# A two-layer decode kernel: projections on the uncentred x, and sums across partitions as two bf16 terms

## The chip, the cores and the metric

The kernel runs on one core of one Trainium2 chip. The metric is the device time of one execution in microseconds (us). Each version is timed in several runs and the median is given. One more execution is recorded by the hardware profiler; its views are what this text calls the profile and the trace.

## What is computed

Four residual steps on x, which has 4 batch rows (one token each) of 512 numbers. Attention A and gated unit B alternate twice, with the same weights and the same K and V both times:

```python
def _layernorm(x, axis=-1, eps=1e-5):
    m = jnp.mean(x, axis=axis, keepdims=True)
    v = jnp.var(x, axis=axis, keepdims=True)
    return (x - m) / jnp.sqrt(v + eps)
...
x = x + A(_layernorm(x))      # q = x @ wq; 32 query heads on 8 K/V heads, 4096 keys, head size 128
x = x + B(_layernorm(x))      # sigmoid(x @ w_gate) * (x @ w_up) @ w_down, inner size 1792
x = x + A(_layernorm(x))
x = x + B(_layernorm(x))
```

Everything is bf16 in memory. K and V are 33.6 MB each and do not fit on the core, so V is read twice and K once, with some of it read again.

## The kernel before

**Layers and batches.** Layer 0 and layer 1 are interleaved: for each batch row b the kernel does attention of layer 0, then `cross` (out-projection result, residual, norm, gated unit, residual, norm), then the queries of layer 1, then the scores of layer 1 on the K tiles that are still in memory. The values of layer 1 follow later, when V comes by a second time. The gated unit of layer 1 is done once for all four rows, in the last `cross`.

**Loads.** All come from SP's queue in the order of a string (line 385): k is two halves of K tiles, V and v a V tile (two halves) for layer 0 and layer 1, r the halves of K that were given up and are read again (`again`, line 386: 3, 3, 2 and 4 halves for the four rows), digits and letters a to d, g, u, w are pieces of the weights, which stay in memory. A half is 512 KB and sits in one of 22 ring slots. A slot comes free when the last reader of its half is done. SP waits for that before it issues the next load.

**K and the scores.** DVE transposes each half of K in place (line 502), 1.234 us each. A batch row's 16 halves, less those read again, stay in their slots from the scores of layer 0 to those of layer 1. Scores (line 515) need the queries spread into block form: PE permutes them (line 478), then four ACT operations write `qbd` (line 491). The softmax takes maxima on DVE (lines 532 to 551), exponentials on ACT (line 556), and transposes the result on PE and ACT into `pt_sb` (line 575).

**Values.** PE multiplies V's halves with `pt_sb` (line 603), 16 matmuls a half. DVE scales by the inverse denominators `winv` into `oT` (line 612). The denominators come from ACT's row sums: two POOL operations (580, 584), a float32 matmul against a column of ones (587), and a reciprocal (589). `y_proj` multiplies by wo.

**The norm.** `layer_norm` and `rstd` (lines 419 to 458): the row sums are summed across partitions by a float32 matmul with a column of -1/512 (`stat`, line 416), DVE adds this negative mean to x and writes bf16 `xT` (440), ACT squares with the mean as bias (445), a second float32 matmul sums across partitions, DVE scales (452), and POOL takes the power -0.5 (456). The matmuls of the gated unit or of q_proj (line 469) take xT. The factor 1/sqrt is applied later, on the results.

**Order of the work.** A planner (`_Sched.place`) lists the operations of each engine by estimated durations and priorities and writes the order out. Every engine then runs its list strictly in that order and waits by semaphores. The durations in `S.put` are the planner's; the priorities are the constants of line 472.

Of the kernel before, what the change touches and what calls it, by code (L numbers as in the profile page):

```python
# [202 lines left out]
def bass_interleave_layers__gqa_block_cached__glu_gated_glu__decode_kernel(nc, A_x, A_k, A_v, A_wq, A_wo, B_x, B_wg, B_wu, B_wd, out):  # L203
# [44 lines left out]
    xT = sb("xT", [P, KD], bf)  # L248
    xTj = sb("xTj", [P, B, KD], bf)
    gs = sb("gs", [P, NF * B])  # L250
    hT = sb("hT", [P, NF * B], bf)
    cols = sb("cols", [P, 64])
    xsum = cols[:, 0:8]
    nmean = cols[:, 8:12]
# [4 lines left out]
    pos, neg, ones, nbias = (cols[:, i:i + 1] for i in range(32, 36))  # L259
# [12 lines left out]
    dsel = sb("dsel", [P, 16])  # L272
# [19 lines left out]

    def col(t):
        return t[:, 0:1].broadcast_to([P, P])
# [23 lines left out]
    for key, ap, v in (("neg", neg, -1.0 / D), ("pos", pos, 1.0 / D), ("mhalf", mhalf, -0.5), ("ones", ones, 1.0)):  # L318
        S.put("dve", lambda e, ap=ap, v=v: e.memset(ap, v), 0.08, 0, writes=[key])
    for name, t in (("mask_a", mask_a), ("sel_den", sel_den)):  # L320
        S.put("pool", lambda e, t=t: e.memset(t[:], 0.0), 0.15, 0, writes=[name, "pl"])
    for g in range(4):
        m = mask_a[32 * g:32 * g + 32, g * R:(g + 1) * R]
        S.put("pool", lambda e, m=m: e.memset(m, 1.0), 0.1, 0, reads=["mask_a"], writes=["mask_a", "sel_den", "pl"])
        v = sel_den[:].rearrange("p (g h) -> p g h", g=4)[:, g, :]
        for a in range(4):
            S.put("pool", affine(sel_den, v, [[-1, R]], -(32 * g + 4 * a), 1.0), 0.2, 0, reads=["sel_den"], writes=["sel_den", "pl"])
# [7 lines left out]
    again = (((6, 1), (7, 0), (7, 1)), ((6, 1), (7, 0), (7, 1)), ((7, 0), (7, 1)), ((6, 0), (6, 1), (7, 0), (7, 1)))  # L335
# [49 lines left out]
    order = 'kk01kk23VkkVVkkVbcdVgaVVVuwrkkkkvkkVvkkVVVVVVVvvvvkvvkrkkvkkkvVkVVVVVVVvvvvkvvrkkkkvkkkvVVVVVVVVvvvvvrvvvvvvvvv'  # L385
    again = (((6, 1), (7, 0), (7, 1)), ((6, 1), (7, 0), (7, 1)), ((7, 0), (7, 1)), ((6, 0), (6, 1), (7, 0), (7, 1)))
# [27 lines left out]
    def stat(c, si, nb, w, wkey, prio):  # L414
        S.put(
            "pe", mm(G_ps[:, c:c + nb], col(w), xsum[:, si:si + nb]), 0.58, prio, reads=[f"xsum{si}", wkey], writes=["G"],
        )

    def layer_norm(x, xkey, xT_ap, xT_key, nb, prio):
        if nb > 1:  # L420
            S.put(
                "dve", lambda e: e.tensor_reduce(xsum[:, 0:nb], x, AX.X, ALU.add), 0.2, prio, reads=[xkey], writes=["xsum0"],
            )
        stat(0, 0, nb, neg, "neg", prio)
        if nb > 1:
            S.put(
                "dve", lambda e: e.tensor_tensor(xw[:], x, bcast(G_ps[:, 0:nb], KD), ALU.add), 0.2, prio,
                reads=[xkey, "G"], writes=["xw"],
            )
            S.put("dve", lambda e: e.tensor_copy(xT_ap, xw[:]), 0.17, prio, reads=["xw"], writes=[xT_key])  # L430
            S.put(
                "dve", lambda e: e.tensor_tensor(xw[:], xw[:], xw[:], ALU.mult), 0.17, prio, reads=["xw"], writes=["xw"],
            )
            S.put(
                "dve", lambda e: e.tensor_reduce(xsum[:, 4:4 + nb], xw[:], AX.X, ALU.add), 0.2, prio, reads=["xw"],
                writes=["xsum4"],
            )
        else:
            S.put(
                "dve", lambda e: e.tensor_scalar(xT_ap, x, G_ps[:, 0:1], None, op0=ALU.add), 0.17, prio,  # L440
                reads=[xkey, "G"], writes=[xT_key],
            )
            S.put("dve", lambda e: e.tensor_copy(nmean[:, 0:1], G_ps[:, 0:1]), 0.15, prio, reads=["G"], writes=["nmean"])  # L443
            S.put(
                "act", lambda e: e.activation(gs[:, 0:KD], x, ACTF.Square, bias=nmean[:, 0:1], accum_out=xsum[:, 4:5]), 0.4,  # L445
                prio, reads=[xkey, "nmean"], writes=["gs", "xsum4"],
            )

    def rstd(mult, rs, rs_key, nb, prio):
        stat(4, 4, nb, pos, "pos", prio)  # L450
        S.put(
            "dve", lambda e: e.tensor_scalar(vpe[:, 0:nb], G_ps[:, 4:4 + nb], mult, mult * eps, op0=ALU.mult, op1=ALU.add),  # L452
            0.17, prio, reads=["G"], writes=["vpe"],
        )
        S.put(
            "pool", lambda e: e.tensor_tensor(rs, vpe[:, 0:nb], mhalf[:, 0:nb], ALU.pow), 0.6, prio,  # L456
            reads=["vpe", "mhalf"], writes=[rs_key, "pl"],
        )

    def q_proj(s, xT_of, n, dst, dkey, prio, xkey):  # L460
        fns = []
        for h in range(16):
            hh = 16 * s + h
            for k in range(KD):
                c0 = (hh % 8) * DH
                fns.append(mm(
                    M_ps[:, h * n:(h + 1) * n], wq[:, hh // 8, k, c0:c0 + DH], xT_of(k), k == 0, k == KD - 1,
                ))
        S.put("pe", fns, 2.0, prio, reads=[xkey, f"wq{2 * s}", f"wq{2 * s + 1}"], writes=["M"])
        S.put("act", lambda e: e.activation(dst, M_ps[:, 0:16 * n], ACTF.Copy), 0.25, prio, reads=["M"], writes=[dkey])  # L470

    PS0, PS1, PL0, PL1, PV0, PV1, PK0, PK1, PDEN, PEV = (1.24, 0.52, 0.5, 1, 1.15, 0.7, 2.1, 2.1, 0.9, 0.6)
# [54 lines left out]
    def softmax(u, rs, rs_key, prio):  # L527
# [11 lines left out]
        S.put("dve", lambda e: e.transpose(tr[:], ml[:]), 0.22, prio, reads=["ml0", "ml1"], writes=["tr"])  # L539
# [28 lines left out]
        for t4 in range(4):  # L568
# [15 lines left out]
            "pool", lambda e: e.tensor_scalar(dsel[:], sel_den[:], ls[:, 0:1], None, op0=ALU.mult), 0.6, pd,  # L584
            reads=["ls0", "sel_den"], writes=["dsel", "pl"],
        )
        S.put("pe", mm(M_ps[:, 480:496], col(ones), dsel[:]), 0.6, pd, reads=["dsel", "ones"], writes=["M"])
# [41 lines left out]
    def cross(l, b, prio):  # L629

        last = l == 1
        nb = B if last else 1
        xres = xj[:] if last else x0[:, b, :]
        y = Y_ps[:, 0:nb * KD]
        u = Y_ps[:, 64:64 + NF * nb]
        g = G_ps[:, 64:64 + NF * nb]
        rs = rs_h[:, 0:nb]
        if last:
            x, xkey, xt = xj[:], "xj", xTj
            S.put(  # L640
                "dve", lambda e: e.tensor_tensor(xj[:], y.rearrange("p (b k) -> p b k", b=nb), xj[:], ALU.add), 0.2, prio,
                reads=["Y", "xj"], writes=["xj"],
            )
            layer_norm(x, xkey, xTj[:], "xTj", nb, prio)
            xk, xtkey = (lambda k: xTj[:, :, k]), "xTj"
        else:
            x, xkey = xj[:, b, :], "xj"
            S.put(
                "dve", lambda e: e.scalar_tensor_tensor(
                    out=x, in0=y, scalar=1.0, in1=xres, op0=ALU.mult, op1=ALU.add, accum_out=xsum[:, 0:1],  # L650
                ), 0.3, prio, reads=["Y", "x0"], writes=["xj", "xsum0"],
            )
            layer_norm(x, xkey, xT[:], "xT", 1, prio)
            xk, xtkey = (lambda k: xT[:, k:k + 1]), "xT"
        for w, key, dst, bkey in ((wg, "wg", g, "G"), (wu, "wu", u, "Y")):
            for f0, f1 in ((0, 3), (3, 6), (6, 10), (10, NF)):
                fns = []
                for f in range(f0, f1):
                    for k in range(KD):
                        fns.append(mm(  # L660
                            dst[:, f * nb:(f + 1) * nb], w[:, k, f * P:(f + 1) * P], xk(k), k == 0, k == KD - 1,
                        ))
                S.put("pe", fns, 0.033 * len(fns), prio, reads=[xtkey, key], writes=[bkey])
                if w is wg and f1 == 6:
                    rstd(4.0, rs, "rs_h", nb, prio)
        if last:
            S.put(
                "dve", lambda e: e.tensor_tensor(
                    gs[:].rearrange("p (f b) -> p f b", b=nb), g.rearrange("p (f b) -> p f b", b=nb),
                    rs.unsqueeze(1).broadcast_to([P, NF, nb]), ALU.mult  # L670
                ), 0.2, prio, reads=["G", "rs_h"], writes=["gs"],
            )
            S.put("act", lambda e: e.activation(gs[:], gs[:], ACTF.Tanh), 0.25, prio, reads=["gs"], writes=["gs"])
        else:
            S.put(
                "act", lambda e: e.activation(gs[:, 0:NF], g, ACTF.Tanh, scale=rs), 0.22, prio, reads=["G", "rs_h"],
                writes=["gs"],
            )
        S.put(
            "dve", lambda e: e.scalar_tensor_tensor(  # L680
                out=hT[:, 0:NF * nb], in0=gs[:, 0:NF * nb], scalar=1.0, in1=u, op0=ALU.add, op1=ALU.mult
            ), 0.2, prio, reads=["gs", "Y"], writes=["hT"],
        )
        fns = []
        for j in range(KD):
            for f in range(NF):
                fns.append(mm(
                    y.rearrange("p (b k) -> p b k", b=nb)[:, :, j], wd[:, f, j * P:(j + 1) * P],
                    hT[:, f * nb:(f + 1) * nb], f == 0, f == NF - 1,
                ))  # L690
        S.put("pe", fns, 1.85, prio, reads=["hT", "wd"], writes=["Y"])
        if not last:
# [159 lines left out]
```

## Time and profile before

| what | value |
|---|---|
| median of 11 runs | 340.29 us (339.05 to 342.87) |
| the profiled execution | 341.07 us |
| its span, first to last instruction | 339.3 us |
| mean granted clock of TensorE | 0.58 |
| HBM read | 120.85 MB |
| busy: PE, DVE, ACT, POOL | 214.9, 147.2, 71.8, 20.4 us |
| K transposes (L502) | 76, 92.8 us in all |
| float32 matmul pairs for sums across partitions | 36, 352 to 366 ns a matmul |

The profile has a page and several views. The page's row of slices cuts the span into 40 equal parts. Groups of instructions give the line, the engine, what is written from what, shapes, a count and the mean time. The chain of waits follows the work that ended last back to its releasers. The timeline lists instructions in order of time; in square brackets stands the idle time of the engine before an instruction, and what ended it. "issue" is idle time in which the engine waited for nothing that the profile shows. L301 is the line of the helper that makes most matmuls, so those are told apart by the tile they write: G_ps, Y_ps and M_ps for the sums, the gated unit and the projections.

### The profile page before, as it was taken

To read this page: it belongs to the slowest core of one execution; us is meant where nothing else is said; L and a number is where in the kernel's file an instruction comes from. 1 tells how busy PE (TensorE), PEld (TensorE's weight loads), DVE (VectorE), ACT (ScalarE), POOL (GpSimd) and SP (SyncE) were. 2 spreads that over 40 slices of the span, in tenths; PEclk is the share of its full clock that TensorE was granted. 3 is DMA by queue.
4 is the path that set the end of the run, shared out by engine and by line. 5 is a ranking of instruction groups with operands and counts; after the bars stand their busy time and mean duration, and the time that the engine had idled before them with its cause. 6 is when DMAs were issued, how large, how long until landed. Compare 5 with 4: busy or idle time off the path is not lost.

```text
span 339.3 us, 11560 instructions
## 1 busy us (share of the span) xinstructions
PE 214.9 (63%) x5202; PEld 162.8 (48%) x5202; DVE 147.2 (43%) x321; ACT 71.8 (21%) x192; POOL 20.4 (6%) x74
## 2 busy tenths in 40 slices
PE   1154633174676668679667586876755868698786
PEld 1123412164633347678223466774332657573676
DVE  6284460000887761012899520134997301155111
ACT  1013103000235303002163230001632200014300
POOL 6100000000001000000000000000000000000001
PEclk9995555555567755555575555555965555557555
DMA  7999999999959999998999999989899999999920
GB/s 216 401 394 410 409 372 381 388 405 371 404 186 375 412 409 408 410 405 312 340 375 396 409 393 409 409 294 352 287 399 412 407 409 408 405 357 308 410 87 4
DMA packets 38626, 121.62 MB, mean 358 GB/s; under 512 B 3504, under 2 KB 9392, under 8 KB 38576
## 3 DMA queue, kind: packets, MB, share of 16 engines
q1 hardware_dynamic: 38544, 120.87, 93.7%
q8 instruction: 41, 0.67, 0.8%
q14 instruction: 9, 0.07, 0.1%
q10 hardware_dynamic: 32, 0.00, 0.0%
HBM read 120.85 MB, written 0.00 MB: 356 GB/s over the span
## 4 chain that ended last, share of the span: by engine, by line
DMA 47%; PE 26%; SPq 11%; DVE 6%; issue 6%; ACT 3%; DVEq 0%; ACTq 0%
DMA ring<-in_A_v_cache_dram 29%; DMA ring<-in_A_k_cache_dram 18%; SPq L341 9%; PE O_ps L603 7%; PE Y_ps L301 5%; PE M_ps L301 5%; PE S_ps L515 5%; PE G_ps L301 3%; DVE ring L502 3%; PE PT_ps L301 2%; SPq L362 1%; DVE ml L532 1%; ACT qbd L491 1%; ACT p_sb L556 1%; ACT p_sb L564 0%
## 5 line engine op out<-in xcount | busy, mean ns | idle before, releaser
L502 DVE STREAM_TRANSPOSE ring<-ring 128x1024 int32<-128x1024 int32 x76 | 92.8, 1234 | 33.2 <-DMA ring<-in_A_k_cache_dram 32.6
L603 PE MATMUL O_ps<-pt_sb,ring 128*128 128x4 bf16 x2048 | 68.2, 167 | 49.9 <-DMA ring<-in_A_v_cache_dram 31.5
L603 PEld LDWEIGHTS O_ps<-pt_sb,ring 128*128 128x128 bf16 x2048 | 63.2, 105 | 61.7 <-DMA ring<-in_A_v_cache_dram 30.8
L515 PE MATMUL S_ps<-ring,qbd 128*16 128x512 bf16 x512 | 53.2, 560 | 8.2 <-DVE ring L502 6.5
L612 DVE TENSOR_TENSOR oT<-O_ps,winv 128x12 bf16<-128x12 f32 (+3 forms) x29 | 4.9, 169 | 73.6 <-PE O_ps L603 73.6
L556 ACT ACTIVATE p_sb<-S_ps,cols 128x512 bf16<-128x512 f32 x32 | 24.7, 773 | 56.3 <-DVE cols L551 48.3
L532 DVE TENSOR_REDUCE ml<-S_ps 128x1 f32<-128x512 f32 x32 | 21.4, 670 | 21.7 <-PE S_ps L515 21.7
L301 PE MATMUL Y_ps<-oT,wo 128*128 128x1 bf16 (+1 forms) x640 | 20.3, 166 | 10.6 <-DMA wo<-in_A_wo_dram 6.9
L515 PEld LDWEIGHTS S_ps<-ring,qbd 128*16 128x16 bf16 x512 | 12.3, 105 | 28.4 <-issue 13.8
L301 PEld LDWEIGHTS Y_ps<-oT,wo 128*128 128x128 bf16 x640 | 18.7, 104 | 12.6 <-DMA wo<-in_A_wo_dram 7.0
L491 ACT ACTIVATE qbd<-M_ps,mask_a 128x64 bf16<-128x64 f32 x64 | 20.1, 314 | 18.5 <-PE M_ps L301 17.0
L445 ACT ACTIVATE gs<-xj,cols 128x4 f32<-128x4 f32 x8 | 2.4, 297 | 83.7 <-DVE cols L443 83.7
L301 PE MATMUL M_ps<-xT,wq 128*128 128x1 bf16 x512 | 15.2, 165 | 6.2 <-issue 3.8
L301 PE MATMUL PT_ps<-ident_b,p_sb 128*128 128x64 bf16 x128 | 10.5, 231 | 12.4 <-ACT p_sb L556 12.4
L301 PEld LDWEIGHTS M_ps<-xT,wq 128*128 128x128 bf16 x512 | 14.5, 104 | 6.8 <-issue 3.9
L301 PEld LDWEIGHTS PT_ps<-ident_b,p_sb 128*128 128x128 bf16 x128 | 7.1, 118 | 17.0 <-ACT p_sb L556 14.3
L456 POOL TENSOR_TENSOR cols<-cols 128x1 f32<-128x1 f32 (+1 forms) x10 | 6.6, 656 | 137.7 <-DVE cols L452 137.5
L564 ACT ACTIVATE p_sb<-PT_ps 128x512 bf16<-128x512 f32 x16 | 9.6, 598 | 17.8 <-PE PT_ps L301 17.8
L301 PE MATMUL G_ps<-cols 128*128 128x1 f32 (+1 forms) x40 | 11.4, 354 | 3.0 <-DVE xj L694 1.0
L580 POOL TENSOR_TENSOR cols<-cols 128x1 f32<-128x1 f32 x16 | 3.1, 193 | 168.9 <-ACT p_sb L556 168.9
L301 PE MATMUL PT_ps<-p_sb,ident_b 128*32 128x128 bf16 x256 | 10.0, 298 | 5.1 <-ACT p_sb L564 3.7
L575 ACT ACTIVATE pt_sb<-PT_ps 128x512 bf16<-128x512 f32 x16 | 9.5, 595 | 15.9 <-PE PT_ps L301 15.9
(75 smaller groups left out, 158.9 us busy)
## 6 DMA issues: line engine op xcount, KB each, us to landing
ring<-in_A_v_cache_dram SPq DMA_DIRECT2D x128, 512.0 KB, 10.4
ring<-in_A_k_cache_dram SPq DMA_DIRECT2D x76, 512.0 KB, 10.3
wq<-in_A_wq_dram SPq DMA_DIRECT2D x4, 1024.0 KB, 13.3
wo<-in_A_wo_dram SPq DMA_DIRECT2D x4, 1024.0 KB, 15.6
wg<-in_B_w_gate_dram SPq DMA_DIRECT2D x1, 1792.0 KB, 11.4
wu<-in_B_w_up_dram SPq DMA_DIRECT2D x1, 1792.0 KB, 17.1
wd<-in_B_w_down_dram SPq DMA_DIRECT2D x1, 1792.0 KB, 21.5
x<-in_A_x_dram SPq DMA_DIRECT2D x1, 4.0 KB, 1.7
```

Source lines behind the costliest of these rows:

```text
L301: return lambda e: e.matmul(o, lhsT=l, rhs=r, start=start, stop=stop)
L341: return e.dma_start(ring[t.slot], t.src.rearrange("(p t) d -> p (t d)", p=P)[:, q * TS:(q + 1) * TS])
L456: "pool", lambda e: e.tensor_tensor(rs, vpe[:, 0:nb], mhalf[:, 0:nb], ALU.pow), 0.6, prio,
L491: "act", lambda e, a=a: e.activation(qbd[u % NQB][:].rearrange("p g n x -> p (g n) x")[:, :, 4 * a:4 * a + 4], M_ps[:, 256:320].rearrange( ...
L502: return e.transpose(v, v)
L515: return e.matmul(bank[32 * gi:32 * gi + 16, :], lhsT=qbd[u % NQB][:, gi, nn, :], rhs=kt[:, :, nn // 2, :, nn % 2], start=nn == 0, stop=nn ...
L532: "dve", lambda e, q=q: e.tensor_reduce(ml[:, q:q + 1], S_ps[banks[q]][:], AX.X, ALU.max, negate=True), 0.65,
L556: "act", lambda e, q=q: e.activation(p_sb[:, 4 * q:4 * q + 4, :].rearrange("p c x -> p (c x)"), S_ps[banks[q]][:], ACTF.Exp, bias=nbias, s ...
L564: "act", lambda e: e.activation(pt1.rearrange("p c g a h -> p (c g a h)"), PT_ps[:], ACTF.Copy), 0.65, prio,
L575: "act", lambda e: e.activation(pt_sb[pi][:].rearrange("p q c g h -> p (q c g h)"), PT_ps[:], ACTF.Copy), 0.65,
L603: return e.matmul(O_ps[:, gi * R:(gi + 1) * R], lhsT=ring[tile.slot][:, (t % HT) * DH:(t % HT + 1) * DH], rhs=pt_sb[pi][:, t % 4, t // 4, ...
L612: "dve", lambda e: e.tensor_tensor(o, O_ps[:, c0:c1], winv[pi][:, c0:c1], ALU.mult), 0.2, PEV,
```

## The change

1. **Projections on the uncentred x.** `xT` holds x itself in bf16, written straight from the matmul result by `add_y`; a second operation writes the float32 x with its sum. For batch row 0 a second column of ones goes through wg, wu and wq, which gives the column sums of the weights (`csum`). `centre` then adds (negative mean) x (column sums) to a projection's result: on the gate, on the up projection and on the queries. The last cross does the same for four rows with broadcasts.
2. **The variance** is taken about the mean of the norm before (`nm`), and corrected by the squared difference of the two means (`dd`).
3. **Sums across partitions** are split: a bf16 copy and the bf16 rest, two matmuls against a bf16 matrix of -1/512. The denominators use it too (`sel_den` holds -512), with two more POOL operations. In a cross, one statistic of both sums stands behind the wg matmuls.
4. **The spread of layer 1's queries** is one DVE product instead of four ACT operations; the copy of q from PSUM on ACT becomes `centre` on DVE.
5. **The order of loads** and the halves read again: 0, 3, 3 and 1 instead of 3, 3, 2 and 4. Three priorities change.

```diff
-    xT = sb("xT", [P, KD], bf)
+    xT = sb("xT", [P, KD, 2], bf)
...
-    for key, ap, v in (("neg", neg, -1.0 / D), ("pos", pos, 1.0 / D), ("mhalf", mhalf, -0.5), ("ones", ones, 1.0)):
+    for key, ap, v in (("negb", negb[:], -1.0 / D), ("mhalf", mhalf, -0.5), ("xT", xT[:], 1.0)):
...
-    order = 'kk01kk23VkkVVkkVbcdVgaVVVuwrkkkkvkkVvkkVVVVVVVvvvvkvvkrkkvkkkvVkVVVVVVVvvvvkvvrkkkkvkkkvVVVVVVVVvvvvvrvvvvvvvvv'
-    again = (((6, 1), (7, 0), (7, 1)), ((6, 1), (7, 0), (7, 1)), ((7, 0), (7, 1)), ((6, 0), (6, 1), (7, 0), (7, 1)))
+    order = '1k0kkkk23VkkVVkVVbdgacVVVuwrvkkkkkkVvkkVVVVVVVvkvvvvkrvkkkkkvvVkVVVVVVVvkvvvvrkkkkkVvvkvkVVVVVVVvvvvvvvvrvvvvvv'
+    again = ((), ((6, 1), (7, 0), (7, 1)), ((5, 1), (6, 1), (7, 1)), ((7, 1),))
...
+    def stat(c, n, prio, reads):
+        hi, lo = (t[:, c:c + n] for t in xs16)
+        S.put("dve", lambda e: e.tensor_copy(hi, xsum[:, c:c + n]), 0.15, prio, reads=reads, writes=["xs_hi"])
+        S.put(
+            "dve", lambda e: e.tensor_tensor(lo, xsum[:, c:c + n], hi, ALU.subtract), 0.15, prio, reads=reads + ["xs_hi"],
+            writes=["xs_lo"],
+        )
+        fns = [mm(G_ps[:, c:c + n], negb[:], hi, True, False), mm(G_ps[:, c:c + n], negb[:], lo, False, True)]
+        S.put("pe", fns, 0.1, prio, reads=["xs_hi", "xs_lo", "negb"], writes=["G"])
...
+    def add_y(b, y, scal, skey, res, rkey, mi, prio):
+        S.put(
+            "dve", lambda e: e.scalar_tensor_tensor(
+                out=xT[:, :, 0], in0=y, scalar=scal, in1=res, op0=ALU.mult, op1=ALU.add,
+            ), 0.2, prio, reads=["Y", rkey] + skey, writes=["xT"],
+        )
+        S.put(
+            "dve", lambda e: e.scalar_tensor_tensor(
+                out=xj[:, b, :], in0=y, scalar=scal, in1=res, op0=ALU.mult, op1=ALU.add, accum_out=xsum[:, 0:1],
+            ), 0.3, prio, reads=["Y", rkey] + skey, writes=["xj", "xsum0"],
+        )
+        S.put(
+            "act", lambda e: e.activation(
+                xw[:, 0, :], xj[:, b, :], ACTF.Square, bias=nm[mi][:, b:b + 1], accum_out=xsum[:, 1:2]
+            ), 0.4, prio, reads=["xj", f"nm{mi}"], writes=["xw", "xsum4"],
+        )
+
+    def norm(b, mi, mult, rs, rs_key, prio):
+        stat(0, 2, prio, ["xsum0", "xsum4"])
+        new, old = nm[1 - mi][:, b:b + 1], nm[mi][:, b:b + 1]
+        S.put("dve", lambda e: e.tensor_copy(new, G_ps[:, 0:1]), 0.15, prio, reads=["G"], writes=[f"nm{1 - mi}"])
...
+    def centre(o, okey, src, skey, n, mi, b, prio):
+        if b == 0:
+            S.put("dve", lambda e: e.tensor_copy(csum[n][:], src[:, :, 1]), 0.2, prio, reads=[skey], writes=[f"cs{n}"])
+        S.put(
+            "dve", lambda e: e.scalar_tensor_tensor(
+                out=o, in0=csum[n][:], scalar=nm[mi][:, b:b + 1], in1=src[:, :, 0], op0=ALU.mult, op1=ALU.add,
+            ), 0.2, prio, reads=[skey, f"nm{mi}", f"cs{n}"], writes=[okey],
+        )
...
-    PS0, PS1, PL0, PL1, PV0, PV1, PK0, PK1, PDEN, PEV = (1.24, 0.52, 0.5, 1, 1.15, 0.7, 2.1, 2.1, 0.9, 0.6)
+    PS0, PS1, PL0, PL1, PV0, PV1, PK0, PK1, PDEN, PEV = (1.24, 0.52, 0.5, 1, 1.15, 0.9, 2.1, 2.1, 0.72, 1.8)
...
-            "pool", lambda e: e.tensor_scalar(dsel[:], sel_den[:], ls[:, 0:1], None, op0=ALU.mult), 0.6, pd,
-            reads=["ls0", "sel_den"], writes=["dsel", "pl"],
-        )
-        S.put("pe", mm(M_ps[:, 480:496], col(ones), dsel[:]), 0.6, pd, reads=["dsel", "ones"], writes=["M"])
+            "pool", lambda e: e.tensor_scalar(dfull[:], sel_den[:], ls[:, 0:1], None, op0=ALU.mult), 0.6, pd,
+            reads=["ls0", "sel_den"], writes=["dfull", "pl"],
+        )
+        S.put("pool", lambda e: e.tensor_copy(dsel[0][:], dfull[:]), 0.6, pd, reads=["dfull"], writes=["dsel0", "pl"])
...
+        fns = [mm(M_ps[:, 480:496], negb[:], dsel[i][:], i == 0, i == 1) for i in range(2)]
+        S.put("pe", fns, 0.1, pd, reads=["dsel0", "dsel1", "negb"], writes=["M"])
...
+    def cross(b, prio):
+        y = Y_ps[:, 0:KD]
+        rs = rs_h[:, 0:1]
+        add_y(b, y, 1.0, [], x0[:, b, :], "x0", 0, prio)
+        n = 2 if b == 0 else 1
+        g, u = glu(n, lambda k: xT[:, k, 0:n], "xT", lambda: norm(b, 0, 4.0, rs, "rs_h", prio), prio)
+        centre(gs[:, 0:NF], "gs", g, "G", "wg", 1, b, prio)
...
+        centre(us_sb[:, 0:NF], "us", u, "Y", "wu", 1, b, prio)
+        down(1, prio)
+        add_y(b, y, rs, ["rs_h"], xj[:, b, :], "xj", 1, prio)
+        norm(b, 1, float(DH), rs_q[1][:, b:b + 1], f"rs_q1{b}", prio)
...
-            q_spread(q2T[s][:], f"q2T{s}", u, prio, ('act', 'act')[1])
+            q_spread(q2T[s][:], f"q2T{s}", u, prio, ('act', 'dve')[1])
```

`glu` holds the wg and wu matmuls as before, with the statistic between them. `last_cross` is the four-row form of `cross`: two operations write `xTj` and `xj`, then come six DVE operations for the sums, `between` with the statistic and the correction, and products with broadcast `csum` and means.

## The prediction

> **What bounds the kernel now.** I read three views of the profile in this order: the page's slices with its DMA queues, the chain that ended last in order of time, then the timeline around one hand-over between the layers. First the page:
>
> ```profile
> DMA  7999999999959999998999999989899999999920
> GB/s 216 401 394 410 409 372 381 388 405 371 404 186 375 412 409 408 410 405 312 340 375 396 409 393 409 409 294 352 287 399 412 407 409 408 405 357 308 410 87 4
> q8 instruction: 41, 0.67, 0.8%
> ```
>
> The transfers run at 405 to 412 GB/s over most of the span, so the load stream is the first bound: a half tile of K or V (0.524 MB) costs 1.27 us at 412 GB/s. The dips come at four places, once per batch, and the last 14 us have no loads at all. The busy time of the stretches shows what the dips cost:
>
> ```profile
> 92.00:106.00 14.00, 11.66 (x182) 5.47 (x182) 11.52 (x19) 6.41 (x20) 1.08 (x3) 0.64 0.73 249
> 154.00:172.00 18.00, 13.80 (x308) 9.33 (x309) 10.56 (x20) 4.89 (x16) 0.55 (x1) 0.55 0.93 317
> 224.00:246.00 22.00, 16.45 (x382) 11.20 (x379) 14.09 (x26) 7.76 (x25) 1.08 (x3) 0.67 0.87 299
> 302.00:312.00 10.00, 9.03 (x153) 4.07 (x150) 3.32 (x10) 3.07 (x9) 0.53 (x2) 0.67 0.94 303
> ```
>
> The columns are the stretch, its length, the busy time of PE, PEld, DVE, ACT and POOL, PE's clock, DMA share and GB/s. Time lost against 412: 14 x (1 - 249/412) = 5.5 us, then 4.2, 6.0 and 2.6. These are hand-overs: batch b's K halves sit in the 22 ring slots until its layer-1 scores, and those wait for cross(0,b) and q_proj. Until then SP waits for a slot, and since it issues in list order, one load without a slot holds all behind it. After the last hand-over the chain holds no load at all:
>
> ```profile
> 274.55 11.44 DMA ring<-in_A_v_cache_dram
> 286.04 0.59 PE O_ps L603 x16
> ...
> 294.60 2.24 issue
> ...
> 320.35 1.42 issue
> ...
> 337.19 0.28 DVE x L711
> ```
>
> So the end is set by (a) when V(0,3,7) lands, just before cross(0,3) starts at 283.75, and (b) some 55 us of arithmetic behind it. The loads end near 324.3. Now the hand-over of batch 1:
>
> ```profile
> 151.81 1.25 DVE L502 STREAM_TRANSPOSE ring<-ring 128x1024 int32<-128x1024 int32 x1 [2.41 <-DMA ring<-in_A_k_cache_dram]
> 152.98 0.18 DVE L694 SCALAR_TENSOR_TENSOR xj<-Y_ps,cols,xj 128x4 f32<-128x4 f32 x1
> 155.28 0.23 DVE L440 TENSOR_SCALAR xT<-xj,G_ps 128x4 bf16<-128x4 f32 x1 [0.94 <-PE G_ps L301]
> 155.57 1.86 PE L301 MATMUL M_ps<-xT,wq 128*128 128x1 bf16 x64
> 158.44 1.35 ACT L491 ACTIVATE qbd<-M_ps,mask_a 128x64 bf16<-128x64 f32 x4 [0.79 <-PE M_ps L301]
> 164.20 0.38 PE L301 MATMUL M_ps<-xT,wq 128*128 128x1 bf16 x9 [2.73 <-issue]
> 164.51 1.89 PE L515 MATMUL S_ps<-ring,qbd 128*16 128x512 bf16 x16
> ```
>
> Two things are to be seen: from the residual (L694) to xT (L440) stand 2.3 us of statistics, and PE stands 2.73 us in the middle of a run of matmuls although its inputs are there ("issue").
>
> **That issue wait is the fetch of PE's program.** Queue q8 brings 0.67 MB in 41 packets, 16 KB each, and PE has 10,404 instructions, 254 to a packet. Counted in the trace, the issue waits of over 1 us on PE end at its instruction 3777, 4289, 5313, 5825, 6081, 6593, 8385, 8641 and 9665: all apart by multiples of 256. Where PE has much to do, such blocks begin at 134.7, 140.9, 147.1, 153.3 and again at 204.1, 210.3, 216.5, 222.7: 6.2 us apart whatever stands in them, while the matmuls of a block need about 128 x 28 ns = 3.6 us (96 of O_ps take 2.72). The Trainium skill ("Runtime: NRT & Kernel Launch", Instruction fetch mechanics) says that a sequencer fetches its next 256 instructions while it runs the current ones, and that the crossing is mostly hidden. By that rule, latency taken out of a hand-over is gained in full; by the row, PE in hand-overs 1, 2 and 3 advances 256 instructions in 6.2 us and a shorter latency mostly becomes a longer issue wait. I follow the row and keep the rule as a rival.
>
> **Part by part.**
>
> *Loads.* The list of second K loads goes from 3+3+2+4 = 12 halves to 0+3+3+1 = 7: 5 x 1.27 = 6.4 us less transfer, 5 x 1.234 us fewer transposes (L502). Of the halves that must land before V(0,3,7), the order string has 198.5 before and 196.5 after (weights counted in halves): 2 fewer, -2.5 us. The other three fall behind it, where the chain holds no loads: worth nothing by themselves.
>
> *Hand-over 0* is not short of instructions: blocks there begin 7 to 9 us apart. L694 to xT is 87.14 to 88.61; the new add_y writes xT straight from Y_ps in one operation like L694's (0.2 us), -1.3. The spread q goes from four ACT operations (1.35 us) to one DVE product of 256 elements: the ends are L612 (0.17 us for 12 elements from PSUM) and L532 (0.67 for 512), and 256 elements lie midway, 0.42; -0.9. One statistic in that chain becomes cheaper too, -0.3: a float32 pair (0.57) becomes two bf16 matmuls (0.2, by the 128x16 row of q2T, 0.18). But K of batch 0 now keeps 16 slots instead of 13: the loads run dry 3 x 1.27 = 3.8 us sooner and restart 2.5 sooner. Stall +1.3; the bounds are 0 (restart as early as the ring runs dry later) and +3.8 (no earlier restart), and I take +1.3, since both terms have rows.
>
> *Hand-overs 1 and 2.* Run-ahead from the last V to a full ring is 21 halves both times in batch 1 and 20 against 19 in batch 2, so slots decide little. Between last V and scores five layer-1 V tiles are listed instead of six: two halves, 2 x 32 = 64 PE instructions, a quarter of a block: 6.2/4 = 1.55 us less fetching each. The latency cuts (-1.9 from L649 to xT, -1.8 from L694 to xT, -0.9 for qbd, +0.2 for centring u: -4.4) I put at nothing beyond that, covered by fetching; were that cover gone they would be worth about 4 each. Bounds 0 and -4.4, taken -1.5 each, by the row of the blocks.
>
> *Up to V(0,3,7)*: -2.5 + 1.3 - 1.5 - 1.5 = -4.2 us.
>
> *Tail.* cross(0,3) and q_proj run at fetch speed (blocks at 284.8, 290.6, 296.8): -0.3. All six remaining V tiles of batch 2 can now fall into it instead of five, up to +1.5; but its loads end earlier (29 halves follow instead of 32), which shortens later fetches: the 1.42 issue wait at 320.4 lies where loads still run, and between 324 and 332 blocks come at 4.5 to 5.9; I take -0.8 for it. Last cross: xT no longer waits for the mean (330.80 becomes about 329.7), but the reciprocal root on POOL (1.04 us, 332.31 to 333.35) then becomes the later input: six DVE operations of 0.17 and two for the split before a statistic after wg, then five of 0.15 to 0.17, give the root at about 333.3; -0.2. Sum -1.3, between +1.5 and -5.
>
> *At no cost, and what hides it.* The reductions of the denominators add two POOL operations (0.19 to 0.33 each) before winv: in the tail L584 ends 311.6, winv is used at 317.5; without that slack +0.6. Moving norm statistics behind the wg matmuls: Square, split, statistic and copy are about 1.9 us against 3 us of wg and wu matmuls; without it 0.3 per cross. Columns of ones in batch 0 widen matmuls from 1 to 2 columns: 128x1 takes 165 ns and 128x4 166. The first norm's four extra DVE operations (0.15 each) and the swap of wq pieces lie before wq's landing, for which PE waits 11 us; 0, at most +0.6 or -1. New constants and priorities alter the planned order; bounded by one 1.25 us transpose per step, either way, in the range.
>
> *Waits added on DVE.* The q2 centring and qbd move from ACT (21% busy) to DVE (43%), and queued behind them are maxima (L532), transposes and oT. They in turn may stand behind a transpose, at most 1.25 us, or behind one that waits for its load, as L694 did above (ready about 150.8, run at 152.98: 2.2).
>
> Total -4.2 - 1.3 = -5.5. Against the profiled run, 341.07 us (339.3 span and 1.8 around it), that is 335.6; the median of the runs is 0.8 lower, 340.29, and I predict 340.3 - 5.5 = 334.8.
>
> **Rivals.**
> *A, as summed (0.53)*: 331.5 to 338, by the bounds of hand-overs 1 and 2.
> *B, fetching is hidden as the page has it (0.15)*: hand-overs 1 and 2 gain 4.2 and 4.4 (of 4.2 and 6.0 that they lose), the tail 4.4: -2.5 + 1.3 - 8.6 - 4.4 - 1.0 = -15.2, so 325, and half of it about 331. For it: the blocks after 153.3 and 222.7 come after 3.9 and 4.0 us, where loads run low. Against: seven steps of 6.2.
> *C, the slots kept for K eat the saving (0.20)*: each of hand-overs 0 to 2 stalls one half longer, not shorter: -2.5 + 3 x 1.27 - 1.3 = 0, so 340.3; at half that stall 338.4. For it: 16 of 22 slots held in batch 0, 15 in batch 3. Against: shorter run-up to scores.
> *D, slower (0.12)*: DVE in its order. If the q2 centring, ahead of the spread and of all layer-1 scores, meets one waiting transpose as L694 did, 2.2 us at each of four hand-overs is +8.8, 340.3 - 5.5 + 8.8 = 343.6. It decides from 5.5/4 = 1.4 us a hand-over. For: 71 transposes of 1.234 us, and DVE waits for K's loads 32.6 us in all. Against: most of those waits lie outside hand-overs 0 and 3.
>
> **How the numbers follow.** About 0.5% (1.7 us) is what a measurement of this kernel can tell from no change. Faster by more than that: A nearly whole (0.50), B (0.15), half of C (0.10): 0.75. Same: the rest of A and most of C, 0.13. Slower: D, 0.12. The range 328 to 341 holds A, C and a part of B's gap, and leaves out D and B's fuller half, 2 in 10.
>
> **What will show it.** Transposes L502 count 71 and HBM reads 118.2 MB. Loads end near 314 to 317, some 20 us before the end, with no load in the chain behind batch 3's last V. Issue waits stay 256 instructions apart and blocks stay at 6.2 us in hand-overs 1 to 3; if they shrink, B holds. The dip near 92 to 106 loses about 7 us; the other two fall to some 3 and 4.5. If the q2 centring or qbd stand behind waiting transposes on DVE, D holds. I am wrong if the load stream's stalls grow by more than the five halves save.

## The result, and the profile after

The changed kernel takes 337.03 us (median of 12 runs, 335.28 to 338.81) against 340.26 us (47 runs of the kernel before): ratio 0.9907, 95% interval 0.9884 to 0.9930. That is 3.2 us faster. 334.8 was forecast, with a range of 328 to 341. The profiled execution took 336.89 us with a span of 335.1, which is 4.2 us below the profiled execution before. The terms below are read from these two executions, so they add up to 4.2 and not to 3.2. A ratio counts, of each kernel, only the runs within 1.5% of its fastest, while a median counts all its runs unless it is called counted. TensorE's granted clock was 0.58 in the profiled execution before and 0.68 in the one after; that does not explain the difference, since in the jobs below the runs of the kernel before at 0.57 to 0.60 and those at 0.67 to 0.71 have medians that differ by 0.8 to 1.1 us, with both signs.

The page of the changed kernel, slices and groups (the helper's line is L304 now):

```profile
GB/s 217 405 399 404 408 393 378 368 407 370 304 65 361 415 409 406 408 409 349 363 405 402 410 408 408 406 351 268 382 410 411 407 409 406 323 244 386 404 120 2
...
HBM read 118.23 MB, written 0.00 MB: 353 GB/s over the span
...
L537 DVE STREAM_TRANSPOSE ring<-ring 128x1024 int32<-128x1024 int32 x71 | 85.7, 1227 | 21.9 <-DMA ring<-in_A_k_cache_dram 21.4
```

The five halves are gone (118.23 MB, 71 transposes). But the dip of hand-over 0 is deeper: a slice of 65 GB/s where 186 was the lowest. The dip near the end is deeper too (323 and 244 where 357 and 308 stood). The windows around the four hand-overs in the changed kernel (last column GB/s):

```profile
86.00:115.00 29.00, 16.29 (x326) 9.16 (x326) 22.56 (x50) 8.21 (x23) 2.44 (x9) 0.92 0.72 267
145.00:190.00 45.00, 32.27 (x710) 20.38 (x710) 31.61 (x70) 11.23 (x29) 3.93 (x14) 0.50 1.01 388
215.00:262.00 47.00, 30.86 (x718) 20.69 (x718) 32.96 (x70) 11.24 (x29) 3.93 (x14) 0.57 0.97 369
285.00:315.00 30.00, 22.95 (x626) 17.39 (x624) 9.73 (x36) 5.74 (x14) 2.75 (x10) 0.56 0.91 331
```

and in the kernel before:

```profile
86.00:115.00 29.00, 19.80 (x359) 11.15 (x355) 25.19 (x44) 11.11 (x32) 1.60 (x5) 0.67 0.88 334
145.00:190.00 45.00, 31.98 (x705) 22.03 (x702) 29.03 (x54) 13.53 (x38) 2.68 (x8) 0.54 0.98 368
215.00:262.00 47.00, 30.64 (x707) 21.89 (x703) 28.79 (x54) 13.63 (x40) 2.69 (x8) 0.61 0.95 355
285.00:315.00 30.00, 23.99 (x587) 18.08 (x585) 11.63 (x32) 7.16 (x22) 1.64 (x4) 0.56 0.99 363
```

Against 412 GB/s these windows lose 10.2, 2.6, 4.9 and 5.9 us in the changed kernel, and 5.5, 4.8, 6.5 and 3.6 in the kernel before. The moments of the hand-overs, from the two timelines (first residual of the cross, second residual, first layer-1 scores), in us:

| | before | changed |
|---|---|---|
| batch 0 | 75.9, 87.1, 94.3 | 75.7, 85.8, 95.2 |
| batch 1 | 142.1, 153.0, 164.5 | 142.0, 150.9, 160.2 |
| batch 2 | 212.6, 224.0, 235.4 | 211.4, 222.9, 231.0 |
| batch 3 | 283.7, 293.3, 303.2 | 280.6, 290.7, 297.7 |
| last cross, end of span | 329.3, 339.3 | 325.7, 335.1 |

The cross of batch 3 starts 3.1 us sooner, and what follows it is 1.1 us shorter (54.5 against 55.6). The chain that ended last, in order of time, in the changed kernel:

```profile
286.27 2.65 issue
288.92 1.55 PE Y_ps L304 x53
...
299.64 6.65 DMA ring<-in_A_k_cache_dram
306.31 1.26 DVE ring L537
307.61 1.91 PE S_ps L550 x14
...
332.99 0.28 DVE x L762
```

There is a load in the tail now. The one half of batch 3's K that is read again was listed behind eight V tiles. It got its slot only when the first scores freed one (SP issues it at 299.64), lands at 306.3, is transposed, and then the last scores start.

### The profile page after: what moved, and what is told of

Same layout as the page of the kernel before. It is cut to its first block, busy times and chain, and to the rows that moved or that the text cites. A ratio compares the mean times of both kernels' runs of the same rounds, so it can differ in the third digit from the quotient of the medians.

```text
span 335.1 us, 11572 instructions
## 1 busy us (share of the span) xinstructions
PE 203.4 (61%) x5184; PEld 149.3 (45%) x5184; DVE 154.3 (46%) x390; ACT 60.2 (18%) x152; POOL 27.1 (8%) x106
## 3 DMA queue, kind: packets, MB, share of 16 engines
HBM read 118.23 MB, written 0.00 MB: 353 GB/s over the span
## 4 chain that ended last, share of the span: by engine, by line
DMA 40%; PE 23%; SPq 15%; issue 11%; DVE 8%; ACT 1%; POOLq 0%; POOL 0%; DVEq 0%; ACTq 0%
DMA ring<-in_A_v_cache_dram 22%; DMA ring<-in_A_k_cache_dram 12%; SPq L344 8%; SPq L365 7%; PE O_ps L644 6%; DMA wd<-in_B_w_down_dram 6%; PE Y_ps L304 6%; PE S_ps L550 5%; PE M_ps L304 4%; DVE ring L537 3%; DVE ml L567 2%; PE G_ps L304 1%; PE PT_ps L304 1%; ACT p_sb L591 0%; DVE tr L574 0%
## 5 line engine op out<-in xcount | busy, mean ns | idle before, releaser
L537 DVE STREAM_TRANSPOSE ring<-ring 128x1024 int32<-128x1024 int32 x71 | 85.7, 1227 | 21.9 <-DMA ring<-in_A_k_cache_dram 21.4
L644 PE MATMUL O_ps<-pt_sb,ring 128*128 128x4 bf16 x2048 | 67.0, 166 | 43.0 <-DMA ring<-in_A_v_cache_dram 30.6
L644 PEld LDWEIGHTS O_ps<-pt_sb,ring 128*128 128x128 bf16 x2048 | 60.9, 104 | 56.4 <-DMA ring<-in_A_v_cache_dram 37.4
L550 PE MATMUL S_ps<-ring,qbd 128*16 128x512 bf16 x512 | 56.0, 580 | 10.7 <-DVE ring L537 8.7
L304 PE MATMUL Y_ps<-oT,wo 128*128 128x1 bf16 (+1 forms) x640 | 20.5, 166 | 13.4 <-DMA wo<-in_A_wo_dram 7.5
L304 PEld LDWEIGHTS Y_ps<-oT,wo 128*128 128x128 bf16 x640 | 18.7, 104 | 15.5 <-DMA wo<-in_A_wo_dram 7.6
L304 PE MATMUL PT_ps<-ident_b,p_sb 128*128 128x64 bf16 x128 | 10.9, 230 | 19.0 <-ACT p_sb L591 19.0
L304 PE MATMUL M_ps<-xT,wq 128*128 128x1 bf16 (+1 forms) x512 | 15.4, 165 | 6.1 <-issue 4.6
L304 PEld LDWEIGHTS PT_ps<-ident_b,p_sb 128*128 128x128 bf16 x128 | 7.2, 116 | 24.6 <-ACT p_sb L591 21.4
L304 PEld LDWEIGHTS M_ps<-xT,wq 128*128 128x128 bf16 x512 | 14.6, 104 | 6.5 <-issue 4.8
L526 ACT ACTIVATE qbd<-M_ps,mask_a 128x64 bf16<-128x64 f32 x32 | 10.0, 313 | 29.2 <-PE M_ps L304 28.5
L465 ACT ACTIVATE xw<-xj,cols 128x4 f32<-128x4 f32 x8 | 2.4, 297 | 70.0 <-DVE xj L460 70.0
L304 PE MATMUL Y_ps<-hT,wd 128*128 128x1 bf16 (+1 forms) x280 | 8.5, 166 | 10.2 <-issue 5.1
L304 PEld LDWEIGHTS Y_ps<-hT,wd 128*128 128x128 bf16 x280 | 8.0, 104 | 10.6 <-issue 8.9
```

Of the source, the lines that this page charges most:

```text
L304: return lambda e: e.matmul(o, lhsT=l, rhs=r, start=start, stop=stop)
L526: "act", lambda e, a=a: e.activation(qbd[u % NQB][:].rearrange("p g n x -> p (g n) x")[:, :, 4 * a:4 * a + 4], M_ps[:, 256:320].rearrange( ...
L537: return e.transpose(v, v)
L550: return e.matmul(bank[32 * gi:32 * gi + 16, :], lhsT=qbd[u % NQB][:, gi, nn, :], rhs=kt[:, :, nn // 2, :, nn % 2], start=nn == 0, stop=nn ...
L644: return e.matmul(O_ps[:, gi * R:(gi + 1) * R], lhsT=ring[tile.slot][:, (t % HT) * DH:(t % HT + 1) * DH], rhs=pt_sb[pi][:, t % 4, t // 4, ...
```

## The experiments

Two theories stood against each other. F: in the hand-overs PE's program fetch sets the pace, 6.2 us for 256 PE instructions, and covers most of the latency taken out. L: that latency pays in full. A third question was where the gain of fewer loads went (S: ring slots). The kernel before took 340.1 to 340.5 us in the same jobs, and 340.0 to 340.1 over the counted runs. Each run has one profile; what is read from it holds for that execution.

| run | us, all runs | us, counted | ratio to before (95%) |
|---|---|---|---|
| loads only | 341.35 (19) | 337.74 (5) | 0.9919 (0.9875 to 0.9962) |
| sums only | 339.45 (22) | 339.45 (22) | 0.9979 (0.9955 to 1.0003) |
| reload earlier | 337.58 (15) | 337.08 (12) | 0.9913 (0.9882 to 0.9944) |
| reloads in batch 0 | 338.16 (22) | 337.72 (17) | 0.9936 (0.9909 to 0.9963) |
| control | 337.29 (6) | 337.29 (6) | 0.9907 (0.9870 to 0.9943) |
| 64 small matmuls | 347.25 (6) | 347.25 (6) | 1.0182 (1.0127 to 1.0237) |
| 8 wide matmuls | 340.06 (22) | 339.00 (14) | 0.9967 (0.9940 to 0.9994) |
| program shifted | 335.61 (6) | 335.61 (6) | 0.9851 (0.9811 to 0.9891) |
| spread on ACT | 339.09 (12) | 339.09 (12) | 0.9968 (0.9936 to 1.0000) |
| shift, reload earlier | 335.16 (6) | 335.16 (6) | 0.9867 (0.9825 to 0.9909) |
| shift, both reloads | 334.25 (6) | 334.19 (5) | 0.9833 (0.9789 to 0.9878) |
| two-term sums only | 340.91 (12) | 340.86 (11) | 1.0032 (0.9996 to 1.0068) |

### Loads only, sums only

The kernel before with the new order string, `again` and constants:

```diff
-    again = (((6, 1), (7, 0), (7, 1)), ((6, 1), (7, 0), (7, 1)), ((7, 0), (7, 1)), ((6, 0), (6, 1), (7, 0), (7, 1)))
+    again = ((), ((6, 1), (7, 0), (7, 1)), ((5, 1), (6, 1), (7, 1)), ((7, 1),))
```

> The kernel before with only the new order of loads, the new list of K halves read again and the three new priorities; norms, sums and spread as before. Theory F (hand-overs run at the pace of PE's program fetch, so shorter arithmetic there is mostly covered): hand-over 0 loses 1 to 2 us more than in the changed kernel, the others hardly more, so about 338 to 340 us. Rival L (latency taken out of a hand-over pays in full, and the new list of loads needs it): with fewer free slots and the long hand-over, the load stream stalls some 3 us more at each of four hand-overs, 345 us or more.

The other half is the changed kernel with the old order string, `again` and constants:

> The changed kernel with the order of loads, the list of K halves read again and the three priorities of the kernel before. Theory F: 120.85 MB read, hand-overs 1 to 3 as long as before within 1.5 us each, hand-over 0 about 2.5 us shorter; 337 to 339.5 us. Rival L: about 4 us less at three hand-overs and in the tail, 326 to 331 us.

What loads alone are worth is not settled: their 19 runs spread over 335 to 344 us, the median of all is 0.8 us above the kernel before (F expected 338 to 340, L 345), and that of the five counted is 2.3 below it. Sums alone give 339.45 us, 0.6 to 1.1 below, at the upper end of F's range and far from L's 326 to 331.

How long a hand-over lasts, from the first residual to the first layer-1 scores, and about how many PE instructions lie in it (both from the traces):

| us, instructions | before | loads only | sums only | changed |
|---|---|---|---|---|
| batch 1 | 22.4, 986 | 18.3, 890 | 18.2, 940 | 18.2, 908 |
| batch 2 | 22.8, 986 | 18.5, 890 | 18.7, 908 | 19.6, 908 |
| batch 3 | 19.5, 922 | 20.0, 954 | 19.3, 876 | 17.1, 876 |

F missed here in part. It expected sums alone to leave the lengths within 1.5 us, and in batches 1 and 2 they fell by 4.2 and 4.1. But the planner also listed fewer value matmuls ahead of the scores in each of these kernels, so the lengths do not tell shorter latency from fewer instructions: before, four blocks of 256 begin inside the stretch of batch 1, and three in each of the others. That either half reaches 18 to 19 us and both get no further agrees with a floor set by the fetch, but does not show one; the shifted kernel below takes 19.2 and 17.5 us for the same 908 instructions. And length is not time: with sums only the windows 145 to 190 and 215 to 262 read 383 and 366 GB/s, so the two hand-overs lose 3.2 and 5.2 us where they lost 4.8 and 6.5.

At hand-over 0 both expectations of F missed. Sums alone, with the old slots, were to make it 2.5 us shorter; second residual to scores takes 7.1 us there and 7.2 before. Loads alone were to lose 1 to 2 us more than the changed kernel; their window 86 to 115 reads 303 GB/s and loses 7.7 us, 2.5 less. So the new arithmetic gains nothing at hand-over 0, even where no issue wait falls into it. Before:

```profile
88.67 1.87 PE L301 MATMUL M_ps<-xT,wq 128*128 128x1 bf16 x64 [0.63 <-DVE cols L443]
90.58 0.18 ACT L470 ACTIVATE q2T<-M_ps 128x16 bf16<-128x16 f32 x1 [1.42 <-PE M_ps L301]
```

and with sums only:

```profile
87.59 1.86 PE L304 MATMUL M_ps<-xT,wq 128*128 128x2 bf16 x64 [0.94 <-DVE xT L455]
91.01 0.23 DVE L491 SCALAR_TENSOR_TENSOR q2T<-csum_q,cols,M_ps 128x16 bf16<-128x16 f32 x1
```

q_proj starts 0.1 us after the second residual instead of 1.5, but its result used to be copied 1.9 us after q_proj began and is now ready for `centre` only after 3.4: `centre` needs the new mean, and that comes through a statistic behind q_proj and a row of DVE operations, some of them behind K transposes.

### 64 small matmuls against 8 wide ones

The direct test of F. Ahead of the wg matmuls of crosses 1 to 3, extra matmuls with equal PE time and equal places in the order, but 128 PE instructions in one case and 16 in the other:

```diff
         add_y(b, y, 1.0, [], x0[:, b, :], "x0", 0, prio)
+        if b > 0:
+            fns = [mm(G_ps[:, 256 + 4 * (i % 32):260 + 4 * (i % 32)], ident_b[:], wq[:, 0, 0, 0:4]) for i in range(64)]
+            S.put("pe", fns, 1.8, prio, reads=["xT", "ident_b", "wq0"], writes=["G"])
```

The wide form has `mm(G_ps[:, 256:512], ident_b[:], wq[:, 0, 0, 0:256])`, 8 times.

> The changed kernel once more, unaltered, as the yardstick for the three runs beside it on the same chip. Both theories: 337.0 us within 0.7.

> The changed kernel with 64 extra matmuls of 4 columns (128 PE instructions, about 1.8 us of PE) ahead of the wg matmuls in crosses 1, 2 and 3; their results go to unused columns. Theory F (hand-overs 1 to 3 run at the pace of the program fetch, 6.2 us for 256 PE instructions): each hand-over 3.1 us longer, 343 to 347 us. Rival L (PE's own time and the waits between operations set the pace): each 1.8 us longer at most, 339 to 342.5 us, the same as with wide matmuls.

> The changed kernel with 8 extra matmuls of 256 columns (16 PE instructions, about 1.7 us of PE) in the place of the 64 small ones; the order of everything else is that of the run with the small ones. Theory F: 0.4 us of fetching each, the PE time falls into the issue waits; 337 to 339 us. Rival L: 1.7 us each, 339 to 342.5 us.

Small: 347.25, or 10.0 us above the control, 3.3 for each hand-over. Wide: 340.06 over all runs and 339.00 counted, 2.8 or 1.7 above. L has both the same. They differ by 7.2 or 8.2 us for 3 x 112 instructions, which is 5.5 or 6.3 us for 256, near the 6.2 of the trace. The wide run lies at or above the upper end of F's 337 to 339, so F's claim that the PE time is absorbed whole is too strong: of 3 x 1.7 us some 1.7 to 2.8 are seen. PE in cross 3 with the small matmuls:

```profile
289.42 1.24 PE L304 MATMUL G_ps<-wq,ident_b 128*128 128x4 bf16 x41 [0.69 <-issue]
...
292.07 0.91 PE L304 MATMUL Y_ps<-xT,wu 128*128 128x1 bf16 x29
295.62 0.86 PE L304 MATMUL Y_ps<-xT,wu 128*128 128x1 bf16 x27 [2.64 <-issue]
```

and with the wide ones:

```profile
282.91 1.87 PE L304 MATMUL G_ps<-wq,ident_b 128*128 128x256 bf16 x8
...
286.16 1.63 PE L304 MATMUL Y_ps<-xT,wu 128*128 128x1 bf16 x56
...
289.66 0.65 PE L644 MATMUL O_ps<-pt_sb,ring 128*128 128x4 bf16 x19 [1.52 <-issue]
```

In the first, wu stops after 29 of 56 matmuls for 2.64 us with nothing to wait for, and the two issue waits end 6.2 us apart (289.42 and 295.62). In the second, wu runs through and the wait comes later and is shorter. The place of the wait goes with the count of instructions, not with the operation.

The DMA packets of queue q8 show the fetch itself. In the kernel before, where blocks begin at 134.7, 140.9 and 147.1, a packet starts 3.6 to 3.7 us after each, takes 1.0 to 1.1, and the next block begins 1.5 us after it has ended: together 6.2 us. After the block of 153.3, in the dip of the loads, the packet starts after 1.1 us and the next block follows after 3.9. What varies is how long the packet waits.

### The program shifted by 200 instructions

In the changed kernel, hand-over 0 has such a wait in the middle of q_proj. Its timeline there:

```profile
85.62 0.22 DVE L455 SCALAR_TENSOR_TENSOR xT<-Y_ps,cols,xj 128x4 bf16<-128x4 f32 x1 [4.48 <-PE Y_ps L304]
...
85.90 1.39 PE L304 MATMUL M_ps<-xT,wq 128*128 128x2 bf16 x46 [0.32 <-DVE xT L455]
...
90.03 0.62 PE L304 MATMUL M_ps<-xT,wq 128*128 128x2 bf16 x18 [2.74 <-issue]
...
92.96 0.39 DVE L520 TENSOR_TENSOR qbd<-M_ps,mask_a 128x256 bf16<-128x256 f32 x1
...
95.20 1.89 PE L550 MATMUL S_ps<-ring,qbd 128*16 128x512 bf16 x16
```

xT is written right behind wd's result in one operation of 0.2 us, as forecast. Then PE stops for 2.74 us after 46 of 64 matmuls. The test puts 100 matmuls of 4 columns at the very start, where PE waits for wq:

```diff
     first_norm(PX)
+    S.put("pe", [mm(M_ps[:, 320:324], ident_b[:], ident_b[:, 0:4]) for _ in range(100)], 2.8, PX, reads=["ident_b"], writes=["M"])
```

> The changed kernel with 100 matmuls of 4 columns (200 PE instructions) at its very start, while PE waits for wq; nothing else. Theory F: the 256-instruction steps move by 200 instructions against the operations; at hand-over 0 the fetch that stopped PE for 2.7 us in q_proj falls into the wait for wd, hand-over 0 loses 2 to 3 us less, 334.5 to 336 us. Rival: the wait belongs to q_proj and its place in the order, it stays, 336.5 to 337.5 us.

335.61 us, 1.7 below the control: more work, less time, as F has it. The same stretch, shifted:

```profile
86.39 1.87 PE L304 MATMUL M_ps<-xT,wq 128*128 128x2 bf16 x64 [0.32 <-DVE xT L455]
...
91.34 0.39 DVE L520 TENSOR_TENSOR qbd<-M_ps,mask_a 128x256 bf16<-128x256 f32 x1
...
93.58 1.89 PE L550 MATMUL S_ps<-ring,qbd 128*16 128x512 bf16 x16
```

q_proj runs whole; residual to scores takes 7.3 us and not 9.4, and the window 86 to 115 (292 GB/s) loses 8.4 us where it lost 10.2. But 7.3 us is what the kernel before needed too (7.2), so the shift takes away the wait and leaves no gain of the arithmetic. Nor is the gain of that window seen in every shifted execution: in the profile of the shift with the reload earlier q_proj runs whole as well, yet wd starts 1.5 us later (85.76) and the window loses 10.0.

The fetch may also explain batch 3, where the changed kernel's hand-over is shorter than that of either half. Counted in the trace, blocks of 256 PE instructions begin at 282.7, 288.9, 293.2 and 296.9 in the changed kernel. The last two steps are 4.3 and 3.7 us instead of 6.2, in a time when the load stream ran low (269 GB/s from 288 to 294). With sums only, where these 6 us read 391 GB/s, they begin at 285.0, 291.2, 296.6 and 300.4, which is 1.2 us more for three steps, of the 2.2 us by which that hand-over is longer. The packets agree: in the changed kernel they start 3.7, 1.9 and 1.1 us after their blocks began, with sums only 3.7, 2.9 and 1.1. With loads only the reading fits less well: there a step of 6.4 us (291.3 to 297.8) lies where the loads had fallen to 339 and 285 GB/s. So it is argued and not shown.

### The slots at hand-over 0

The changed kernel with `again[0] = ((6, 1), (7, 0), (7, 1))`:

> The changed kernel with three K halves of batch 0 read again as in the kernel before, which leaves the ring 9 free slots instead of 6 at hand-over 0 and reads 1.6 MB more. Theory S (the free slots decide how long the load stream runs dry at hand-over 0): the loss there falls from 9.5 us to about 5, which pays for the 3.8 us of extra loads, 336.5 to 337.5 us, no change within 0.5 us. Rival: the hole is made by the 2.9 us issue wait of PE in q_proj, the same slots or not; then the extra loads are all cost, 340 to 341 us.

338.16 us (337.72 counted), 0.4 to 0.9 above the control: a little above S, and well below the rival's 340. The window says more:

```profile
86.00:115.00 29.00, 18.42 (x326) 9.68 (x326) 25.35 (x56) 8.47 (x23) 2.44 (x9) 0.80 0.88 335
```

335 GB/s and not 267: the loss falls from 10.2 to 5.4 us, and 3.8 us of loads come back. PE's wait in q_proj is still there (its next block begins at 90.04), so the wait did not make the hole, as the rival had it. Three slots more are worth 4.8 us of stall, three halves less are worth 3.8 us of transfer, and they cancel within what the runs can tell. S holds for the hole; the changed kernel's saving of three reads in batch 0 bought nothing that can be seen.

### The reload in the tail

```diff
-    ...vkvkVVVVVVVvvvvvvvvrvvvvvv'
+    ...vkvkVVVVVVVvvvvvvrvvvvvvvv'
```

> The changed kernel with the one K half of batch 3 that is read again moved ahead of two V tiles of layer 1 (order ends vvvvvvrvvvvvvvv instead of vvvvvvvvrvvvvvv). Theory: in the changed kernel that load found no free slot until the first scores of layer 1, landed at 306 us and held the last scores about 3 us; moved, it lands before the scores and the end comes 2 to 3 us sooner, 334 to 335 us. Rival: the end is held by the last V tiles or by the program fetch all the same, 336.5 to 337.5 us.

337.58 us (337.08 counted), level with the control: the rival's number. In its profile the wait is gone:

```profile
300.49 1.25 DVE L537 STREAM_TRANSPOSE ring<-ring 128x1024 int32<-128x1024 int32 x1 [1.07 <-DMA ring<-in_A_k_cache_dram]
...
304.28 1.89 PE L550 MATMUL S_ps<-ring,qbd 128*16 128x512 bf16 x16
```

First scores to last cross take 26.7 us instead of 28.0. But cross 3 began 2.0 us later in that execution, at 282.6, although all engines' orders up to there are the changed kernel's. So the reload's wait is real, 1.3 us in one profile, and its worth in time is not shown. It stays open.

### The other parts, and the best version

> The changed kernel with the spread of layer 1's queries back on ACT (four operations, 1.35 us, in place of one DVE product of 0.4 us). Theory F: hand-overs 1 to 3 are covered by the program fetch, hand-over 0 is 0.3 to 1 us longer; 337 to 338 us. Rival L: 1 us at each of four hand-overs, 340.5 to 341.5 us.

339.09 us, 1.8 above the control (which ran in another job). F expected up to 1 in all and L 3.5 or more: neither is met. In its profile the four hand-overs last 19.9, 18.4, 19.5 and 17.2 us against 19.5, 18.2, 19.6 and 17.1 in the changed kernel, so hand-over 0 is 0.4 longer and the others hardly differ, as F has it; but cross 0 starts 1.5 us later there, ahead of any spread of layer 1. Where the 1.8 us come from stays open.

> The kernel before with only its sums across partitions and its denominators as two bf16 terms (two more DVE operations ahead of each norm statistic, two more POOL operations for each denominator, two short matmuls instead of a float32 pair). Theory F: nothing, 339.5 to 341 us, since the number of PE instructions is the same. Rival (PE time counts): 36 pairs of 0.57 us become 0.2 us, 13 us less of PE, of which the hand-overs' part is seen: 336 to 338 us.

340.91 us: as F has it, the two-term sums by themselves gain nothing, although each pair saves some 0.4 us of PE.

> The changed kernel with the 100 matmuls at the start and the last K half read again ahead of two V tiles. Theory: the shift is worth 1.7 us as measured, the earlier load takes 1 to 2 us out of the tail, 333.5 to 335 us. Rival: the earlier load is worth nothing, as its own run said, 335 to 336 us.

> As the run before, and also with three K halves of batch 0 read again. Theory S: at hand-over 0 more slots and 3.8 us of extra loads about cancel, within 1 us of the run without them: 333 to 336 us. Rival (with the issue wait gone from hand-over 0, its hole is smaller and the extra loads are cost): 337 us or more.

335.16 and 334.25 us. The first lies in both of its expectations and decides nothing. The second is as S has it and beats both kernels, ratio 0.9833 (0.9789 to 0.9878), though the steps among the three shifted versions lie within their spread. Its window 86 to 115 reads 340 GB/s and loses 5.1 us; without the slots, in the run before it, the window reads 270 and loses 10.0.

## Why the prediction was right, and where its terms were not

Direction and size held (3.2 us of 5.5). The reason given for the modest size, PE's program fetch, is shown by the small and wide matmuls, by the packets and by the shift. The rule of the Trainium skill that was weighed ("Runtime: NRT & Kernel Launch", Instruction fetch mechanics: the crossing is mostly hidden) does not hold for this kernel; 10.0 against 1.7 to 2.8 us for the same PE time decides. That the sum came out so near owes something to luck: hand-over 0 cost 3.4 us more than its term, and the loads and hand-over 1 gained 1.8 more than theirs. Against the profiled executions, term by term:

- **Loads ahead of V(0,3,7), -2.5**: the list has two halves fewer. By the start of cross 3, 1.5 MB fewer had moved (105.7 and 104.3 MB, by the DMA packets of the two traces), which is nearly three halves, 3.6 us. With loads only, cross 3 starts at 280.0, as early as in the changed kernel.
- **Hand-over 0, +1.3, is the step that failed**: measured +4.7. The stall term (+3.8 for three slots) was right in kind and too low: giving them back took 4.8 off. The -2.5 for a sooner restart did not come, and not for one cause. The 2.74 us issue wait fell into q_proj and moved the first scores from 94.3 to 95.2; I had called this hand-over "not short of instructions" from its spacing before, and it was one fetch away from being so. But without that wait the arithmetic gains nothing either (second residual to scores 7.1 us with sums only, 7.3 shifted, 7.2 before): the sum counted what xT, the statistic and the spread save, and put at nothing that the queries now wait for the mean in `centre`.
- **Hand-overs 1 and 2, -1.5 each**: measured -2.2 and -1.6. The number is right, but its working is not shown: PE's instructions in the stretch fell by 78 where the step counted 64, and the 4.4 us of latency taken as covered cannot be told from them, since sums alone shortened both hand-overs by 4 us.
- **Tail, -1.3**: measured -1.1, but by other terms. Cross 3 to scores -2.4 and not -0.3; last cross -0.6 and not -0.2; scores to last cross +1.9, of which the late reload's wait is 1.3 in one profile, where I had no load in the chain at all. That the -1.3 came out is luck. "Worth nothing by themselves" was right of the three halves behind V(0,3,7), but that the one remaining half, listed too late, costs something was missed. Loads end at 321.9, not at 314 to 317.
- **At no cost**: the two-term denominators and sums cost nothing measurable (their own run is +0.8 us, with 1 inside its interval).
- Ahead of cross 3 the measured terms and -0.4 in the stretches between are -3.6 + 4.7 - 2.2 - 1.6 - 0.4 = -3.1, as the residuals show. Single executions of the same program differ by 2 us at that point, as the earlier reload showed.

Two readings in the prediction were off. The last load of the chain before lands at 285.99 (274.55 and 11.44), 2.2 us after cross(0,3) had started, so it is not V(0,3,7) but a later V tile that PE takes up inside that cross. And A's lower end, 331.5, does not follow from the bounds of -4.4, which give 329.0.

Of the rivals, B (fetching is hidden) is out by the small and wide matmuls and by the packets. C had the right place and cause at hand-over 0, where the slots cost 4.8 us and not 1.3, and was wrong for hand-overs 1 and 2. D's mechanism came in small: at hand-over 0 of the changed kernel the qbd product stands some 0.75 us behind a transpose (91.80 to 93.04); in the shifted one the copy of the mean stands behind another as well. It did not decide the sign.

## What to carry to other kernels

Where PE works through many short matmuls while loads keep the DMA engines full, count its instructions. Here 128 more of them in a hand-over cost 3.3 us where the same PE time in 16 cost 0.6 to 0.9, and moving the block boundary to where the engine waits anyway gained 1.7. When an operation is moved off a chain, list what its successor now waits for: q_proj started earlier, and its result waited for the mean. A tile kept in memory saves its second read but takes a slot from the load stream; at hand-over 0 the two cancelled (3.8 against 4.8 us), so each kept tile has to be priced where the stream runs dry.

## What the runs showed of the hardware that was not expected

Starting PE's program with 100 needless matmuls made the kernel 1.7 us faster. A block of 256 PE instructions follows the one before in 6.2 us where PE has much to do and the loads run full (203.1, 209.3, 215.5, 221.7 in the changed kernel) and mostly in 3.7 to 4.6 where loads run low. At one place it takes far longer: the block that began at 79.55 was followed by the next only at 90.03, and its packet started 8.0 us after the block began, where it was 2.9 in the kernel before. In the profiles of the control and of the runs with small and wide matmuls it is 7.8 to 8.0 as well, so this is no accident of one execution. Why that packet comes so late stays open.
